# Sign bits of an LSH attention kernel: twelve full-width split matmuls or four narrow fp32 ones, with a new order of all work

## The chip, the cores and the metric

The kernel runs on one core of a Trainium2 chip. The metric is the device time of one execution in microseconds, as the median of several runs. A profiled execution has a time of its own and a span, from its first to its last instruction, in which the trace counts.

## The reference

Four batches of eight heads attend over 768 positions with head dimension 64. A query sees a key only if both fall into the same of 64 buckets; a bucket is the six sign bits of the vector's projection by `proj` (64x6). The attention result, laid side by side over heads, is `x` of a second stage with cosine and sine mixing over tokens and a rectified linear layer.

```python
q_bits = (np.einsum('bhsd,dk->bhsk', q, proj) > 0)      # k_bits alike, from k
mask = q_bucket[:, :, :, None] == k_bucket[:, :, None, :]
scores = np.where(mask, scale * q @ k.T, -1e9)
attn = softmax(scores); x = attn @ v                    # heads side by side
theta = x @ w_theta
y = w_tok_r @ (x * cos(theta)) + w_tok_i @ (x * sin(theta))
u = x + y
out = u + maximum(u @ w_ch, 0)
```

## The kernel before, in words

Work is cut into small operations (`op(...)`) that carry a priority, the engines that may run them and what they depend on. `issue_all` (L111) walks a model of the five engines and gives every engine one list, which it then runs strictly in that order. The priorities come from named constants at the end of the file (L1044 to L1100). A duration in an `op` is the model's and not a measured one.

Heads are worked in pairs; there are sixteen pairs. The steps of a pair that matter here:

- **Load and split** (`prep_qk`, L544). `raw` tiles of q and k, 128 rows (two heads of 64) by 768 positions, come in by DMA (L556). Each is split for exact products into a rounded high part (L563 on ScalarE or L565 on VectorE) and the remainder (L569 on GpSimd or VectorE), both in tile `hl`.
- **Sign bits** (`bits`, L583). `proj` stands, split alike, in four 128x128 tiles `pst` (filled once, L329 and L330), in columns 0 to 23 for q and 32 to 55 for k, each with its negative. TensorE adds three products (high by high, low by high, high by low) for q and three for k into one 128-row PSUM tile `pb`, once for positions 0 to 511 and once for 512 to 767: twelve matmuls in a pair. VectorE makes the bits from rows 0 to 55 with one comparison for each of the two tiles (`rows`, L594). For the very first head it also writes them straight into the operands (L598).
- **Assembly** (`assemble`, L633). SyncE's queue issues six DMAs for a head's `qt` and `kt` operands from `hl` (L640 to L644) and two for its bit rows from `rows` (L648, L649). There are three sets of operands in turn, so a head's assembly waits for the last score matmul of the head three before.
- **Maxima** (`maxima`, L665): matmuls `sq`, a maximum on VectorE (`mc`, L691), a transpose `pmx`, a row sent back by DMA (L715) and a flag row `ft` (L720).
- **Steps** (`step`, L735): score matmuls `st`, the exponential `pf` (L769) and its rounded copy (L775) on ScalarE, the remainder `p` on GpSimd (L781), and products with v into `po`. The matmuls of `po` stream 64 or 65 columns each.

The second stage of a batch (`moe`, L833) is laid between the attention of the next one: `pt_x` and `ps_th` (angles), `py` (token mixing), `pt_u` and `ps_r` (the last layer). For the last batch nothing is left to lay it between. Weights are prepared once, in the first 300 us. All matmuls but the transposes go through the helper `mm`, so their line is L76.

Of the kernel before, what the change touches and what calls it, by code (L numbers as in the profile page):

```python
# [14 lines left out]
F32 = mybir.dt.float32  # L15
# [16 lines left out]
def lsh_attention_moe_kernel(ctx: ExitStack, tc: tile.TileContext, q, k, v, proj, w_theta, w_tok_r, w_tok_i, w_ch, aff, out):  # L32
# [6 lines left out]
    P = 128  # L39
# [30 lines left out]
    for nm in "qk":  # L70
        for part in "hl":
            pst[nm, part] = const.tile([P, P], F32R, name=f"pst_{nm}{part}")
            DVE.memset(pst[nm, part].bitcast(F32), 0.0)
# [10 lines left out]
    SHARED = {"p1", "p2", "zf", "zh", "zl", "mag", "wlow", "whigh", "wmul", "wl", "vv2"}  # L84
# [26 lines left out]
    def issue_all():  # L111
# [96 lines left out]
        while todo:  # L208
            progress = False
            for e in START:  # L210
# [28 lines left out]
                if e == "PE":  # L239
                    dur = pace(now, dur, STREAM.get(o.name, 0.9))  # L240
                elif e == "DVE" and o.name in SHARED:
                    port[0] = max(now, port[1]) + dur
                    dur = port[0] - now
                elif e == "POOL":
                    port[1] = max(now, port[0]) + dur
                    dur = port[1] - now
                elif e == "SP":
                    t_ = now
                    for hold, size in dur:
                        t_ += 25 + hold  # L250
# [48 lines left out]
    def on(e, dur, fn):  # L299
        return {e: (dur, fn)}  # L300
# [21 lines left out]
    def split_proj():  # L322
        for nm, base, first in (("q", 0, 1.0), ("k", 32, -1.0)):
            for j in range(2):
                rows = slice(j * D, (j + 1) * D)
                for n, sgn in enumerate((first, -first)):
                    c0 = base + j * 2 * NB + n * NB
                    h_, l_ = (pst[nm, part][rows, c0 : c0 + NB] for part in "hl")
                    DVE.tensor_scalar(h_, pp[rows, :], sgn, None, ALU.mult)  # L329
                    DVE.scalar_tensor_tensor(l_, pp[rows, :], sgn, h_.bitcast(F32), ALU.mult, ALU.subtract)  # L330

    cload = op("consts", QKL + 0.03, on("SP", [(625, 0)] * 3, load_consts))
    proj_ready = op("pst", QK0, on("DVE", 2200, split_proj), [cload])
# [210 lines left out]
    def prep_qk(b, hp, G, g):  # L544
        t = {}
        sh, sr = Slot("hl"), Slot("rows")
        raws = []
        hs, ls = [], []
        pr = G + at("QK0", b)
        for i, src in enumerate((q, k)):  # L550
            def part(i=i, src=src):
# [25 lines left out]
        fs = []  # L577
        for lo, n_ in ((0, 512), (512, S - 512)):
            def signs(lo=lo, n_=n_):
                sm_ = Slot("m")  # L580
                u = {}

                def bits():  # L583
                    u["pb"] = bank(sm_, [P, 512], f"pb_{b}_{hp}_{lo}")
                    n = 0
                    for i, nm in enumerate("qk"):
                        for a_, c in (("h", 0), ("h", 1), ("l", 0)):
                            mm(u["pb"][:, :n_], pst[nm, a_], t["hl"][:, c, i, lo : lo + n_], n == 0, n == 5)
                            n += 1

                def sign():
                    if "rows" not in t:
                        t["rows"] = ap_.tile([56, S], F32R, tag=sr.tag, bufs=1, name=f"rows_{b}_{hp}")
                    DVE.tensor_scalar(t["rows"][:, lo : lo + n_], u["pb"][:56, :n_], affs[:56, 0:1], affs[:56, 1:2], ALU.is_ge, ALU.mult)  # L594

                def first():
                    for r0, dst in ((0, qts[0]), (32, kts[0])):
                        DVE.tensor_scalar(  # L598
                            dst[MR : MR + NM, 0, lo : lo + n_], u["pb"][r0 : r0 + NM, :n_], affs[r0 : r0 + NM, 0:1], affs[r0 : r0 + NM, 1:2], ALU.is_ge, ALU.mult
                        )  # L600

                b1 = op("bits", G + at("QK1", b), on("PE", 80 + 1340 * n_ / 512, bits), hs + ls + [proj_ready], [sm_, sh])
                if g == 0:
                    t.setdefault("direct", []).append(op("sign0", G + at("QK1", b) - 0.01, on("DVE", 2 * (190 + 540 * n_ / 512), first), [b1], [sm_]))
                fs.append(op("sign", G + at("QK1", b), on("DVE", 190 + 540 * n_ / 512, sign), [b1], [sm_, sr]))

            signs()

        t["parts"], t["bits"], t["slots"] = hs + ls, fs, [sh, sr]
        if g == 0:  # L610
# [10 lines left out]
            t["first"] = list(t["direct"])  # L621
# [11 lines left out]
    def assemble(j, n_, t, prio, free_after):  # L633
        h0 = j * D
        qf, kf = qts[n_].bitcast(F32), kts[n_].bitcast(F32)

        hq, hk = (lambda i=i: t["hl"][:, :, i].bitcast(F32) for i in range(2))

        def parts():
            dma(qf[:D], hq()[h0 : h0 + D, 0:1].to_broadcast([D, 2, S]))  # L640
            dma(kf[:D], hk()[h0 : h0 + D])
            for c in range(2):
                dma(qf[D : D + hd, c], hq()[h0 + c * hd : h0 + (c + 1) * hd, 1])  # L643
                dma(kf[D : D + hd, c], hk()[h0 + c * hd : h0 + (c + 1) * hd, 0])  # L644

        def bits():
            rf = t["rows"].bitcast(F32)
            dma(qf[MR : MR + NM, 0], rf[j * NM : (j + 1) * NM])  # L648
            dma(kf[MR : MR + NM, 0], rf[32 + j * NM : 32 + (j + 1) * NM])  # L649

        n = S * 4
        sh, sr = t["slots"]
        return [
            op("assemble", prio, on("SP", [(1000, 4 * D * n)] * 2 + [(1000, 2 * hd * n)] * 4, parts), t["parts"] + free_after, [sh]),
            op("assbits", prio + AB, on("SP", [(780, NM * n)] * 2, bits), t["bits"] + free_after, [sr]),
        ]
# [383 lines left out]
CL = 0.33  # L1040
# [3 lines left out]
MX0 = -3.263  # L1044
MX1 = 0.411
PIECES = [{1: (0, 3)}, {0: (0, 2), 1: (2, 3)}]
PF = 0.112
KA = 0.401
KB = 0.749
KV = 0.529  # L1050
KN = 1.258
AB = -0.043
WTH = 16.998
WTS = 0.232
WC = 27.543
# [8 lines left out]
TH0_3 = -0.791  # L1064
TH1_3 = 0.535
Y0_3 = 11.712
YS_3 = 4.023
Y1_3 = 0.838
MX0_0 = -3.0
MX1_0 = 0.299  # L1070
AS0_0 = -5.786
PV0_0 = -4.367
QK0_0 = -7.07
QK1_0 = -5.655
HOLD = 0.255
LATE = 6
WL0 = 33.637
WLS = 3.314
TH0_0 = -0.032
TH1_0 = 0.837  # L1080
Y0_0 = 8.598
Y1_0 = 2.702
YS_0 = 4.448
AHEAD = 2.344
QKL = -10.187
QKI = 0.127
QKH = [(0, 999, ["ACT", "DVE"])]
QKLO = [(0, 999, ["POOL", "DVE"])]
QK0 = -5.533
QK1 = -4.662  # L1090
AS0 = -4.539
PV0 = -4.161
LV0 = -5.392
W0 = 0.383
WS = 3.307
TH0 = 0.02
TH1 = 0.742
Y0 = 8.953
YS = 5.502
Y1 = 2.736  # L1100
# [4 lines left out]
def _thresholds(n):  # L1105
# [41 lines left out]
```

## Time and profile before

| | |
|---|---|
| time before, median of 3 runs | 856.34 us (855.6 to 857.42) |
| the profiled execution's own time | 857.2 us |
| its span | 855.4 us |
| mean granted TensorE clock | 0.954 |
| busy: TensorE, VectorE, ScalarE, GpSimd | 794.8, 570.4, 520.9, 497.1 us |
| matmuls of the sign bits | 192 (sixteen pairs by twelve) |

A group line of the profile reads: line, engine, operation, output<-inputs, shapes, count, then busy time and mean duration of one, then the idle time of the engine before them and what ended it. PE is TensorE's matmuls, PEld its weight loads, DVE VectorE, ACT ScalarE, POOL GpSimd and SPq the queue that issues DMAs. Matmuls overlap in the records, so the pace of a row of matmuls is read from start to start and not from durations. A timeline row gives start, length of the merged group, engine, what it is and the count. The chain of waits is the work that ended last, followed back.

### The profile page before, as it was taken

How to read it: one execution, taken by the hardware profiler on the slowest of the kernel's cores; microseconds unless marked ns; L12 is line 12 of the kernel's file. 1: busy time of each engine (PE TensorE's matmuls, PEld its weight loads, DVE VectorE, ACT ScalarE, POOL GpSimd, SP SyncE). 2: the span in 40 equal slices, each digit the busy share in tenths (PEclk: the TensorE clock that was granted, in tenths of full speed). 3: DMA queues.
4: the chain of work that ended last, by engine and by line, in shares of the span. 5: the costliest groups of instructions: out<-in, count | busy, mean ns of one | idle time of the engine just before them, and what ended most of it. 6: DMA issues, size and time to landing. Idle time of an engine off the chain costs nothing.

```text
span 855.4 us, 17719 instructions
## 1 busy us (share of the span) xinstructions
PE 794.8 (93%) x6808; PEld 566.4 (66%) x6808; DVE 570.4 (67%) x962; ACT 520.9 (61%) x888; POOL 497.1 (58%) x511
## 2 busy tenths in 40 slices
PE   3799988899898899999999999999999999999997
PEld 2477766678556676778667766778667766675465
DVE  7999988786898755575896455575796445235413
ACT  3289867777797345467977444476876453657200
POOL 3199976974768545475778544574678543641200
PEclk8599996979899999999999999999999999999999
DMA  7566773753235414344343423252343321000001
GB/s 224 145 194 173 202 180 90 167 130 70 74 81 131 106 41 108 69 100 101 78 93 79 122 53 95 58 134 66 78 93 83 82 47 42 14 14 1 0 21 55
DMA packets 33781, 79.01 MB, mean 92 GB/s; under 512 B 6520, under 2 KB 10808, under 8 KB 33696
## 3 DMA queue, kind: packets, MB, share of 16 engines
q1 hardware_dynamic: 33696, 77.88, 35.8%
q8 instruction: 54, 0.88, 0.4%
q14 instruction: 31, 0.25, 0.1%
HBM read 32.51 MB, written 6.29 MB: 45 GB/s over the span
## 4 chain that ended last, share of the span: by engine, by line
PE 65%; DVE 14%; ACT 9%; SPq 3%; issue 3%; DMA 3%; POOL 3%; DVEq 0%; ACTq 0%; POOLq 0%
PE py L76 18%; PE st L76 12%; PE po L76 9%; PE ps_r L76 8%; PE sq L76 6%; PE ps_th L76 5%; DVE mc L691 3%; PE pb L76 2%; POOL p L781 2%; ACT pf L769 2%; DVE hl L569 2%; ACT p L775 2%; PE pt_u L870 1%; SPq L644 1%; SPq L643 1%
## 5 line engine op out<-in xcount | busy, mean ns | idle before, releaser
L781 POOL TENSOR_TENSOR p<-pf,p 128x512 f16<-128x512 f32 x288 | 357.6, 1263 | 193.5 <-ACT p L775 118.6
L769 ACT ACTIVATE pf<-st 128x512 f32<-128x512 f32 x288 | 164.1, 593 | 132.7 <-PE st L76 123.3
L691 DVE TENSOR_REDUCE mc<-sq 128x1 f32<-128x512 f32 (+1 forms) x288 | 191.1, 681 | 61.9 <-PE sq L76 60.7
L76 PE MATMUL py<-z,wtk 128*128 128x512 f16 x864 | 222.4, 385 | 1.2 <-POOL z L959 0.8
L76 PE MATMUL st<-qt,kt 108*128 108x512 f32 (+3 forms) x768 | 201.1, 378 | 8.1 <-ACT pf L769 7.9
L775 ACT ACTIVATE p<-pf 128x512 f16<-128x512 f32 x288 | 171.8, 628 | 10.7 <-PE po L76 7.7
L76 PEld LDWEIGHTS <-p 128*128 128x128 f16 x3456 | 136.4, 100 | 44.9 <-issue 19.0
L76 PE MATMUL po<-vv,p 128*128 128x65 f16 (+1 forms) x3456 | 158.3, 197 | 6.2 <-POOL p L781 6.1
L76 PE MATMUL sq<-kt,qt 108*128 108x256 f32 (+1 forms) x384 | 137.4, 415 | 21.0 <-DVE mc L691 14.7
L76 PEld LDWEIGHTS st<-qt,kt 108*128 108x128 f32 (+1 forms) x768 | 124.1, 201 | 29.7 <-ACT pf L769 16.2
L76 PEld LDWEIGHTS <-wtk 128*128 128x128 f16 x864 | 71.5, 99 | 86.7 <-issue 26.9
L76 PEld LDWEIGHTS sq<-kt,qt 108*128 108x128 f32 x384 | 70.0, 201 | 45.5 <-DVE mc L691 25.8
L959 POOL TENSOR_TENSOR z<-f,z 128x512 f16<-128x512 f32 x38 | 50.9, 1347 | 49.9 <-ACT z L953 37.4
L948 DVE SCALAR_TENSOR_TENSOR f<-x,zsc,z 128x512 f32<-128x512 f32 x48 | 58.9, 1266 | 9.9 <-ACT z L936 7.3
L76 PE MATMUL ps_th<-wth,h_x 128*128 128x512 f32 x192 | 63.7, 414 | 1.1 <-DVE z L914 0.8
L76 PE MATMUL ps_r<-wch,h_u 128*128 128x512 f32 x192 | 63.3, 411 | 0.8 <-ACT h_u L875 0.7
L994 DVE SCALAR_TENSOR_TENSOR x<-ps_r,x 128x512 f32<-128x512 f32 x24 | 16.6, 691 | 57.3 <-PE ps_r L76 57.3
L875 ACT ACTIVATE h_u<-pt_u 128x512 fp32r<-128x512 f32 x24 | 14.2, 595 | 62.9 <-PE pt_u L870 62.7
L76 PEld LDWEIGHTS ps_th<-wth,h_x 128*128 128x128 f32 x192 | 36.4, 195 | 10.7 <-DVE z L914 1.2
L76 PEld LDWEIGHTS ps_r<-wch,h_u 128*128 128x128 f32 x192 | 35.5, 191 | 9.6 <-ACT h_u L875 0.9
L76 PE MATMUL ps_th<-wth,l_x 128*128 128x512 f32 x96 | 38.9, 406 | 0.1
L76 PE MATMUL ps_r<-wch,l_u 128*128 128x512 f32 x96 | 38.3, 399 | 0.0
(131 smaller groups left out, 935.6 us busy)
## 6 DMA issues: line engine op xcount, KB each, us to landing
qt<-hl SPq DMA_DIRECT2D x31, 384.0 KB
kt<-hl SPq DMA_DIRECT2D x31, 384.0 KB
raw<-in_q_dram SPq DMA_DIRECT2D x16, 384.0 KB
raw<-in_k_dram SPq DMA_DIRECT2D x16, 384.0 KB
vb<-in_v_dram SPq DMA_DIRECT2D x16, 384.0 KB
out_dram<-x SPq DMA_DIRECT2D x24, 256.0 KB
qt<-hl SPq DMA_DIRECT2D x62, 96.0 KB
kt<-hl SPq DMA_DIRECT2D x62, 96.0 KB
```

The costliest lines, as they stand in the source:

```text
L76: PE.matmul(out_, l, r, start=start, stop=stop, skip_group_check=True)
L569: return lambda: eng.tensor_tensor(t["hl"][:, 1, i], t["raw", i], t["hl"][:, 0, i].bitcast(F32), ALU.subtract)
L643: dma(qf[D : D + hd, c], hq()[h0 + c * hd : h0 + (c + 1) * hd, 1])
L644: dma(kf[D : D + hd, c], hk()[h0 + c * hd : h0 + (c + 1) * hd, 0])
L691: DVE.tensor_reduce(col()[:, cs], u["sq"], AX.X, ALU.max)
L769: ACT.activation(wide("pf", spf, F32), u["st"], AF.Exp, scale=1.0 / math.sqrt(D))
L775: ACT.activation(o_, u["pf"], AF.Copy)
L781: return lambda: eng.tensor_tensor(wide("p2", sp2, F16), u["pf"], u["p1"], ALU.subtract)
L875: ACT.activation(u["hi"], u["pt"], AF.Copy)
L948: DVE.scalar_tensor_tensor(u["f"], tl[b][:, tt], zsc[:, b : b + 1], t["zw"][r][:, tt], ALU.mult, ALU.mult)
L959: return lambda: eng.tensor_tensor(t["z"][r, 1][:, tt], u["f"], t["z"][r, 0][:, tt], ALU.subtract)
L994: DVE.scalar_tensor_tensor(tl[b][:, to], r_["ps"], 0.0, tl[b][:, to], ALU.max, ALU.add)
```

## The change

The sign bits no longer use the split tiles. `pst` becomes one plain fp32 tile of 32 columns for q and one for k. Four plain fp32 matmuls read the loaded `raw` tiles, one for each of q and k and each half of 384 positions, and write 32 rows each at partitions 0, 32, 64 and 96 of one PSUM tile. One comparison of 128x384 replaces the two of 56x512 and 56x256. The two halves of the positions now stand in different rows of `rows`, so a head's bits go out in four DMAs of 12x384 instead of two of 12x768. The matmuls wait for the two loads and no longer for the split; in return the `raw` buffers are held until the matmuls have read them.

The planner counts a score or projection matmul that stands behind a short one as dearer, and the lists of all engines are made anew with other priority constants; of those, two lines are shown.

```diff
-        for part in "hl":
-            pst[nm, part] = const.tile([P, P], F32R, name=f"pst_{nm}{part}")
+        pst[nm] = const.tile([P, 32], F32, name=f"pst_{nm}")
...
+        def key(o, e):
+            if e == "PE" and tail_pe in SHORT and o.name in FOUR:
+                return (o.key[0] + PEN, o.key[1])
...
-                    DVE.tensor_scalar(h_, pp[rows, :], sgn, None, ALU.mult)
-                    DVE.scalar_tensor_tensor(l_, pp[rows, :], sgn, h_.bitcast(F32), ALU.mult, ALU.subtract)
+                    DVE.tensor_scalar(pst[nm][rows, c0 : c0 + NB], pp[rows, :], sgn, None, ALU.mult)
...
-                    for i, nm in enumerate("qk"):
-                        for a_, c in (("h", 0), ("h", 1), ("l", 0)):
-                            mm(u["pb"][:, :n_], pst[nm, a_], t["hl"][:, c, i, lo : lo + n_], n == 0, n == 5)
-                    DVE.tensor_scalar(t["rows"][:, lo : lo + n_], u["pb"][:56, :n_], ...)
-                b1 = op("bits", ..., hs + ls + [proj_ready], [sm_, sh])
+            for x in range(2):
+                for i, nm in enumerate("qk"):
+                    r0 = 64 * x + 32 * i
+                    mm(t["pb"][r0 : r0 + 32], pst[nm], t["raw", i][:, x * SH : (x + 1) * SH], True, True)
+            DVE.tensor_scalar(t["rows"], t["pb"], affs[:, 0:1], affs[:, 1:2], ALU.is_ge, ALU.mult)
+        b1 = op("bits", ..., raws + [proj_ready], [sm_] + nats)
...
-            dma(qf[MR : MR + NM, 0], rf[j * NM : (j + 1) * NM])
-            dma(kf[MR : MR + NM, 0], rf[32 + j * NM : 32 + (j + 1) * NM])
+            for x in range(2):
+                for r0, dst in ((64 * x, qf), (64 * x + 32, kf)):
+                    dma(dst[MR : MR + NM, 0, x * (S // 2) : (x + 1) * (S // 2)], rf[r0 + j * NM : r0 + (j + 1) * NM])
...
-AB = -0.043
+AB = 0.151
```

Three places show how the lists move. First, VectorE near its start. `pst` is the projection, `kt` and `qt` are the first head's operands, `vam` is a maximum of v, and `pb` and `affs` stand for the sign operation. Before, these rows follow on fourteen more `pst` rows of the same two kinds:

```order
L329 TENSOR_SCALAR pst_kh<-pp 64x6
L330 SCALAR_TENSOR_TENSOR pst_kl<-pp,pst_kh 64x6
L618 CAST kt_116<-hl_0_141 64x1536
L618 CAST qt_113<-hl_0_141 32x768 x2
L618 CAST kt_116<-hl_0_141 32x768
L453 TENSOR_REDUCE vam_0_189<-vb_0_139 128x1
L598 TENSOR_SCALAR qt_113<-pb_0_0_172,affs 12x512
L598 TENSOR_SCALAR kt_116<-pb_0_0_172,affs 12x512
L594 TENSOR_SCALAR rows_0_203<-pb_0_0_172,affs 56x512
```

Now these are the rows at that place:

```order
L336 TENSOR_SCALAR pst_q<-pp 64x6 x4
L336 TENSOR_SCALAR pst_k<-pp 64x6 x4
L459 TENSOR_REDUCE vam_0_159<-vb_0_135 128x1
L621 CAST kt_112<-hl_0_137 64x1536
L621 CAST qt_109<-hl_0_137 32x768 x2
L621 CAST kt_112<-hl_0_137 32x768
L602 TENSOR_SCALAR qt_109<-pb_0_154,affs 12x384
L602 TENSOR_SCALAR kt_112<-pb_0_154,affs 12x384
```

Eight `pst` operations stand there instead of sixteen, the maximum of v has moved ahead of the copies, and the sign operations still come last.

Second, the queue of DMAs where the fourth head is assembled, `qt_113` with `kt_116` before and `qt_109` with `kt_112` now; `hl` and `rows` are the sources, `vb` is a load of v and `w_t` are loads of the token weights. Before:

```order
L648 DMA qt_113<-rows_1_315 12x768
L649 DMA kt_116<-rows_1_315 12x768
L640 DMA qt_113<-hl_1_250 64x2x768
L641 DMA kt_116<-hl_1_250 64x2x768
L643 DMA qt_113<-hl_1_250 32x768
L644 DMA kt_116<-hl_1_250 32x768
L643 DMA qt_113<-hl_1_250 32x768
L644 DMA kt_116<-hl_1_250 32x768
```

Now:

```order
L643 DMA qt_109<-hl_1_234 64x2x768
L644 DMA kt_112<-hl_1_234 64x2x768
L646 DMA qt_109<-hl_1_234 32x768
L647 DMA kt_112<-hl_1_234 32x768
L646 DMA qt_109<-hl_1_234 32x768
L647 DMA kt_112<-hl_1_234 32x768
L455 DMA vb_2_590<-in_v_dram 128x2x384
L364 DMA w_t_599<-in_moe_w_tok_r_dram 128x1536
L364 DMA w_t_599<-in_moe_w_tok_i_dram 128x1536
L653 DMA qt_109<-rows_1_314 12x384
L653 DMA kt_112<-rows_1_314 12x384
L653 DMA qt_109<-rows_1_314 12x384
```

The bit rows have moved from the head of this assembly to its end, behind three loads, and a fourth of them follows.

Third, TensorE at the end of the program: `pt_u` transposes a block of u, `ps_r` is the last layer on it, from the parts `h_u` and `l_u` and the weights `wch`; blocks are numbered 0 to 5. Before:

```order
L76 MATMUL ps_r_4_11853<-wch_104,h_u_4_11842 128x512
L76 MATMUL ps_r_4_11853<-wch_103,l_u_4_11843 128x512
L870 MATMUL pt_u_5_11867<-ident,x_9159 128x128 x4
L76 MATMUL ps_r_5_11878<-wch_103,h_u_5_11873 128x512
L76 MATMUL ps_r_5_11878<-wch_104,h_u_5_11873 128x512
```

Now:

```order
L75 MATMUL ps_r_2_11703<-wch_100,h_u_2_11671 128x512
L75 MATMUL ps_r_2_11703<-wch_99,l_u_2_11672 128x512
L874 MATMUL pt_u_4_11718<-ident,x_9081 128x128 x4
L874 MATMUL pt_u_5_11724<-ident,x_9081 128x128 x4
L75 MATMUL ps_r_3_11732<-wch_99,h_u_3_11700 128x512
L75 MATMUL ps_r_3_11732<-wch_100,h_u_3_11700 128x512
```

The last transpose has moved ahead of the matmuls of three blocks; before, it stood ahead of those of its own block alone.

More of the change, by code (lines that the diff above doesn't have):

```diff
@@ L70, in lsh_attention_moe_kernel @@
     for nm in "qk":
-        for part in "hl":
-            pst[nm, part] = const.tile([P, P], F32R, name=f"pst_{nm}{part}")
-            DVE.memset(pst[nm, part].bitcast(F32), 0.0)
+        pst[nm] = const.tile([P, 32], F32, name=f"pst_{nm}")
+        DVE.memset(pst[nm], 0.0)
     def mm(out_, l, r, start, stop):
@@ L322, in split_proj @@
     def split_proj():
-        for nm, base, first in (("q", 0, 1.0), ("k", 32, -1.0)):
+        for nm, first in (("q", 1.0), ("k", -1.0)):
             for j in range(2):
@@ L326, in split_proj @@
                 for n, sgn in enumerate((first, -first)):
[L327 to L330, printed above, removed]
+                    c0 = j * 2 * NB + n * NB
+                    DVE.tensor_scalar(pst[nm][rows, c0 : c0 + NB], pp[rows, :], sgn, None, ALU.mult)
     cload = op("consts", QKL + 0.03, on("SP", [(625, 0)] * 3, load_consts))
-    proj_ready = op("pst", QK0, on("DVE", 2200, split_proj), [cload])
+    proj_ready = op("pst", QK0, on("DVE", 700, split_proj), [cload])
     wth = [wp.tile([P, NC, DM], F32R, name=f"wth{i}") for i in range(2)]
@@ new lines, in prep_qk, with bits, sign @@
+        sm_ = Slot("m")
+        SH = S // 2
+        def bits():
+            t["pb"] = bank(sm_, [P, SH], f"pb_{b}_{hp}")
+            for x in range(2):
+                for i, nm in enumerate("qk"):
+                    r0 = 64 * x + 32 * i
+                    mm(t["pb"][r0 : r0 + 32], pst[nm], t["raw", i][:, x * SH : (x + 1) * SH], True, True)
+        def sign():
+            t["rows"] = ap_.tile([P, SH], F32R, tag=sr.tag, bufs=1, name=f"rows_{b}_{hp}")
+            DVE.tensor_scalar(t["rows"], t["pb"], affs[:, 0:1], affs[:, 1:2], ALU.is_ge, ALU.mult)
@@ new lines, in first @@
+        def first():
+            for x in range(2):
+                for r0, dst in ((64 * x, qts[0]), (64 * x + 32, kts[0])):
+                    DVE.tensor_scalar(
+                        dst[MR : MR + NM, 0, x * SH : (x + 1) * SH], t["pb"][r0 : r0 + NM], affs[r0 : r0 + NM, 0:1], affs[r0 : r0 + NM, 1:2], ALU.is_ge, ALU.mult
+                    )
+        b1 = op("bits", G + at("QK1", b), on("PE", 1000, bits), raws + [proj_ready], [sm_] + nats)
+        direct = []
+        if g == 0:
+            direct.append(op("sign0", G + at("QK1", b) - 0.01, on("DVE", 4 * 470, first), [b1], [sm_]))
@@ L609, in prep_qk @@
+        fs = [op("sign", G + at("QK1", b), on("DVE", 570, sign), [b1], [sm_, sr])]
         t["parts"], t["bits"], t["slots"] = hs + ls, fs, [sh, sr]
@@ L619, in copy @@
                 return go
-            t["first"] = list(t["direct"])
+            t["first"] = list(direct)
             pieces = [
@@ L1063 @@
 SEED = 162248
[L1064 to L1075, printed above, removed]
-LATE = 6
[L1077 to L1086, printed above, removed]
+TH0_3 = -0.906
+TH1_3 = 0.619
+Y0_3 = 6.012
+YS_3 = 1.533
+Y1_3 = 0.094
+MX0_0 = -2.821
+MX1_0 = 0.312
+AS0_0 = -3.257
+PV0_0 = -4.336
+QK0_0 = -10.002
+QK1_0 = -6.235
+HOLD = 0.008
+LATE = 6
+WL0 = 17.76
+WLS = -31.029
+TH0_0 = 0.005
+TH1_0 = 0.805
+Y0_0 = 8.965
+Y1_0 = 1.355
+YS_0 = 5.682
+AHEAD = 1.962
+QKL = -12.217
+QKI = 1.196
 QKH = [(0, 999, ["ACT", "DVE"])]
 QKLO = [(0, 999, ["POOL", "DVE"])]
[L1089 to L1100, printed above, removed]
+QK0 = -5.81
+QK1 = -5.002
+AS0 = -1.218
+PV0 = -4.271
+LV0 = -3.122
+W0 = -0.514
+WS = 3.131
+TH0 = -0.21
+TH1 = 0.948
+Y0 = 8.868
+YS = 5.812
+Y1 = 2.817
 _INS = ["q", "k", "v", "proj", "moe_w_theta", "moe_w_tok_r", "moe_w_tok_i", "moe_w_ch"]
```

76 lines of the change are left out of this document (32 added, 44 removed).

## The prediction

> **What bounds the kernel now.** I read the page's busy shares first, then the windows by stretch, then the chain of waits.
>
> ```profile
> PE 794.8 (93%) x6808; PEld 566.4 (66%) x6808; DVE 570.4 (67%) x962; ACT 520.9 (61%) x888; POOL 497.1 (58%) x511
> ```
>
> ```profile
> 0.00:24.00 24.00, 9.46 (x25) 5.91 (x25) 19.30 (x50) 8.48 (x8) 7.85 (x20) 0.82 0.67 200
> 24.00:290.00 266.00, 234.33 (x2150) 175.06 (x2150) 232.64 (x371) 202.36 (x353) 199.48 (x193) 0.88 0.52 137
> 290.00:760.00 470.00, 462.33 (x4205) 331.70 (x4203) 281.76 (x494) 279.67 (x484) 278.08 (x291) 0.99 0.32 77
> 760.00:856.00 96.00, 88.67 (x432) 53.73 (x432) 36.73 (x49) 30.41 (x44) 11.66 (x9) 1.00 0.05 17
> ```
>
> The columns behind the stretch are its length and the busy time of PE, PEld, DVE, ACT and POOL, then the granted clock. From 290 to 760 us TensorE is busy for 462.33 of 470 us (98%) and the others for about 60%: a microsecond taken off TensorE there is a microsecond off the end. From 24 to 290 us TensorE has 88%, VectorE 87%, at a clock of 0.88: two engines share the bound. In the first 24 us VectorE leads with 19.30.
>
> ```profile
> PE 65%; DVE 14%; ACT 9%; SPq 3%; issue 3%; DMA 3%; POOL 3%; DVEq 0%; ACTq 0%; POOLq 0%
> ```
>
> The chain agrees: two thirds TensorE, and VectorE mostly at the start.
>
> **The sign-bit matmuls, old price.** Sixteen pairs; the same windows for tile `pb` alone give twelve matmuls in the first stretch, 72 in the second, 108 in the third, so one, six and nine pairs.
>
> ```profile
> 0.00:24.00 24.00, 3.93 (x12) 2.99 (x12) 4.02 (x6) 0.82 0.67 200
> 24.00:290.00 266.00, 16.00 (x72) 12.20 (x72) 7.71 (x12) 0.88 0.52 137
> 290.00:760.00 470.00, 22.66 (x108) 17.45 (x108) 11.81 (x18) 0.99 0.32 77
> ```
>
> A pair at full clock, from TensorE's timeline, with what follows it:
>
> ```profile
> 590.06 0.62 PE L76 MATMUL pb<-hl,pst_qh 128*128 128x512 f32 x2
> 590.53 0.40 PE L76 MATMUL pb<-hl,pst_ql 128*128 128x512 f32 x1
> ...
> 591.80 0.40 PE L76 MATMUL pb<-hl,pst_kh 128*128 128x256 f32 x2
> 592.04 0.28 PE L76 MATMUL pb<-hl,pst_kl 128*128 128x256 f32 x1
> 592.16 0.60 PE L870 MATMUL pt_x<-ident,x 128*128 128x128 f32 x4
> ```
>
> From 590.06 to 592.16 is 2.10 us a pair. A 256-column matmul takes 0.12 us of it from start to start (591.80 to 592.04 for two).
>
> **New price.** No row shows a plain fp32 matmul of 32 output columns. The nearest is `pm`, plain fp32 with 33 output columns over 128 streamed ones.
>
> ```profile
> L76 PE MATMUL pm<-vb,ones x32: 272/297/425, 25.2 to 695.8; 128*33 128x128 f32 x32
> L76 PEld LDWEIGHTS pm<-vb,ones x32: 107/110/161, 25.2 to 695.7; 128*33 128x33 f32 x32
> 51.94 0.41 PE L76 MATMUL pm<-vb,ones 128*33 128x128 f32 x2
> ```
>
> There are 32 records for sixteen calls (one a pair), so a plain fp32 matmul is two instructions. The two together last 0.41 us and one lasts 0.297, so the second starts 0.113 us after the first: 128 columns take what 256 take in the split form. For 384 columns that is 0.34 us an instruction, and a pair has eight. If nothing overlaps, a pair takes 8 x 0.34 = 2.7 us, 0.6 more than now. If the four narrow matmuls, which write separate quarters of the partitions, run beside each other, it takes 2 x 0.34 = 0.68 us. If they start strictly in list order, and only the second instruction of each must wait for its first, the steps are five: 1.7 us. I take 1.2 us, the middle of the two overlapping cases, since the four share no output rows and wait for one another in nothing that the diff shows; that they overlap at all is shown by no row, and the other end is a rival below.
>
> The Trainium skill ("TensorE: Matmul & The Clock Gate", Part 3, "Measured speedup vs the span model") states 2.38 times for three column tiles of 32. By it four would give some 3.2 times, an estimate: 0.85 us a pair, and 837 us for the whole; no row here shows it.
>
> **What the saving is worth.** 2.1 - 1.2 = 0.9 us a pair. Nine pairs count in full; six lie where VectorE binds as much as TensorE, and I count half; the first one belongs to the start. That is 12 x 0.9 = 10.8 us off, and between 17 off (0.68) and 7 on (2.7).
>
> **VectorE.** One comparison for two, and fewer preparations.
>
> ```profile
> L594 DVE TENSOR_SCALAR rows<-pb,affs 56x512 fp32r<-56x512 f32 x16 | 12.8, 797 | 10.9 <-PE pb L76 10.8
> L594 DVE TENSOR_SCALAR rows<-pb,affs 56x256 fp32r<-56x256 f32 x16 | 8.5, 529 | 2.6 <-PE pb L76 2.6
> ```
>
> Between 529 ns for 256 and 797 for 512, 384 columns take 0.66; a pair goes from 1.33 to 0.66. After 290 us VectorE's idle 40% hides that; before, it is in the half that I counted. At the start it is on the path, first by its timeline, then by the chain:
>
> ```profile
> 5.68 0.16 DVE L329 TENSOR_SCALAR pst_qh<-pp 64x6 fp32r<-64x6 f32 x1
> ...
> 9.90 0.16 DVE L330 SCALAR_TENSOR_TENSOR pst_kl<-pp,pst_kh 64x6 fp32r<-64x6 f32 x1
> 10.09 0.95 DVE L618 CAST kt<-hl 64x1536 fp32r<-64x1536 f32 x1
> ...
> 12.67 0.95 DVE L453 TENSOR_REDUCE vam<-vb 128x1 f32<-128x768 f32 x1
> 13.66 0.80 DVE L598 TENSOR_SCALAR qt<-pb,affs 12x512 fp32r<-12x512 f32 x1
> ```
>
> ```profile
> 37.24 2.82 PE pwt L424 x12
> ```
>
> VectorE works without a break from 5.68, and in the chain it stays the main carrier up to the first weight transposes. Sixteen `pst` operations take 5.68 to 10.09, 4.4 us; eight at 0.19 from start to start (9.90 to 10.09) take 1.5, so 2.9 us go. The four direct sign operations keep their sum (twice 797 and twice 529 before, four times 660 now). The comparisons of the first two pairs give 0.67 each. Together 4.2; I take 4 us. New on the path could be the first bits themselves:
>
> ```profile
> 8.70 1.19 PE L76 MATMUL pb<-hl,pst_qh 128*128 128x512 f32 x2 [8.70 <-DVE pst_qh L329]
> ...
> 12.35 0.28 PE L76 MATMUL pb<-hl,pst_kl 128*128 128x256 f32 x1
> ```
>
> At that clock the pair takes 3.9 us, 1.87 times 2.1. With `pst` done at 7.2, bits of 1.2 x 1.87 = 2.2 us end at 9.4, while the copies and the maximum of v hold VectorE until 10.7: hidden. At 2.7 x 1.87 = 5.1 they end at 12.3, and 1.6 of the 4 us is lost.
>
> **The new order on TensorE.** A wide weight load behind short matmuls shows:
>
> ```profile
> 492.16 0.71 PE L76 MATMUL st<-qt,kt 108*128 108x512 f32 x2
> 492.70 0.63 PE L76 MATMUL pb<-hl,pst_qh 128*128 128x512 f32 x2
> ```
>
> Behind `po`, the two `st` take 0.54 us; two `pb` in a dense stream took 0.47 (590.06 to 590.53). So 0.07 us at each such place. The lists have 231 of them before; now 200, and eight more behind the new bits: 23 fewer, 1.6 us off. At the end the last block:
>
> ```profile
> 847.00 0.60 PE L870 MATMUL pt_u<-ident,x 128*128 128x128 f32 x4
> ...
> 848.29 0.73 PE L76 MATMUL ps_r<-wch,h_u 128*128 128x512 f32 x2 [0.69 <-ACT h_u L875]
> ...
> 849.01 0.50 PE L76 MATMUL ps_r<-wch,l_u 128*128 128x512 f32 x1
> ```
>
> TensorE idles 0.69 us ahead of the block's first matmul, and the third comes 0.72 after it where 0.47 is usual: 0.9 us of waiting for the split of u. Now the matmuls of two more blocks, 24 of 0.23 us, lie between that transpose and this block, 5.6 us in which the split is done, and the 0.9 goes. What else the new constants move I count as zero.
>
> **SyncE's queue.** Two more DMAs for each of 31 heads:
>
> ```profile
> 410.68 0.77 SPq L648 DMA_DIRECT2D qt<-rows  x1
> 411.51 0.72 SPq L649 DMA_DIRECT2D kt<-rows  x1
> ```
>
> The first and the last of four heads whose assembly is in the chain of waits, how long `sq` waited for bit rows, and what the `raw` loads wait for:
>
> ```profile
> 89.51 1.22 SPq L643
> ...
> 325.49 1.22 SPq L643
> ```
>
> ```profile
> L76 PE MATMUL sq<-kt,qt 108*128 108x512 f32 x192 | 91.4, 493 | 11.5 <-DVE mc L691 8.3 <-DVE kt L598 1.5 <-DMA kt<-rows 1.2
> ```
>
> ```profile
> SPq L556 <- DVE hl L569: 67.1, 13, 13.3
> ```
>
> One costs 0.8 us with its gap, so an assembly takes 1.6 us longer, and where the bits now come last, behind loads, the first `sq` of the head waits for that; the row and flag DMAs of other heads stand behind it. The cost lies between nothing, since `sq` waited 1.2 us on `rows` in the whole run, and 31 x 1.6 = 50. If the four heads in the chain all stay there, it is 6.4 us. TensorE idles for only 7.7 us from 290 to 760, so most of the 6.4 is covered by other work; I take 2 us. The `raw` loads get one more reader to wait for, TensorE, with the rest of the queue behind them; they already wait 67.1 us for the remainders on VectorE, which read the same tile, so I cost that at nothing; without this cover, a load comes later by TensorE's lag behind the split.
>
> **Sum.** -10.8 - 4 - 1.6 - 0.9 + 2 = -15.3. The profiled execution's own time is 857.2, its span 855.4 and 1.8 around it, which stays; 841.9. It lies 0.9 above the median shown, so 841 us.
>
> **Rivals.**
> - *Nothing overlaps (slower).* The eight instructions of a pair run one behind another: 12 x (2.7 - 1.2) = 18, and 1.6 at the start: 860.6. It decides when a pair costs over 1.2 + 15.3 / 12 = 2.5 us. For it: no row shows two matmuls beside each other. If besides no weight load were hidden, 8 x 0.11 (the `pm` load) add 0.9 a pair, 871. Against that last part:
>
> ```profile
> L76 PEld LDWEIGHTS pb<-hl,pst_qh x64: 187/190/339, 8.7 to 686.4; 128*128 128x128 f32 x64
> ```
>
>   Loads of 0.19 us would bring twelve matmuls to over 4 us a pair, and they took 2.10: the loads are hidden, though all use the full 128 rows. The Trainium skill (the same page and part, "The mechanism") has it that a weight load overlaps a running matmul only if their row groups differ; the trace speaks against it.
> - *The queue is late.* If eight of the heads assembled before 290 us each lose 1.6 us, 12.8 stands for my 2: 852. For it: bits at the end of an assembly; against: the 1.2 us.
> - *The order gives it back.* If the new lists lose the 2.5 us of the two order terms and double TensorE's 7.7 us of idling, it is 851.
>
> **How the numbers follow.** Overlap, 0.65: 835 (0.68 us a pair) to 847 (1.7), likeliest 841. Nothing overlaps, 0.13, of which 0.02 at 871. Queue, 0.10. Order, 0.12. The range is 830 to 857: the overlap case with some microseconds for the order either way, and both cases at 851 and 852; it leaves out nearly all of the slow rival and a few hundredths below. A measurement can tell about 0.2%, 1.7 us. Faster by more: 0.65, and most of the queue and order cases with a little of the slow one, 0.20, together 0.85. Same: 0.05. Slower: 0.10, from the slow rival.
>
> **What would show it.** Right: `pb` from its first start to the next matmul takes about 1.2 us at full clock, with starts nearer together than 0.34; VectorE reaches the first sign operation some 3 us before 13.66; the gap ahead of the last `ps_r` is gone; TensorE is still at 98% from 290 us on. Wrong: eight `pb` records at 0.34 us from start to start, `sq` rows idle behind DMAs from `rows`, or more idle TensorE from 290 us to the last batch's second stage than 8 us.

## The result and the profile after

| | before | after |
|---|---|---|
| median of the runs | 855.97 us (4 runs, 854.99 to 857.42) | 831.0 us (4 runs, 829.88 to 832.03) |
| profiled execution: own time, span | 857.2, 855.4 us | 829.88, 827.8 us |
| TensorE idle in the span | 60.6 us | 59.8 us |

The ratio of after to before is 0.9707, 95% interval 0.9686 to 0.9727: 25.0 us faster, where 15.3 were forecast. The time lies in the range, 1 us inside its fast end.

The busy times of the engines over the whole span of after:

```profile
PE 768.0 (93%) x6744; PEld 532.5 (64%) x6744; DVE 562.5 (68%) x940; ACT 519.4 (63%) x889; POOL 497.8 (60%) x506
```

TensorE went from 794.8 us to 768.0, 26.8 off, and its idle time stayed. Almost the whole difference of the spans, 27.6, is TensorE's busy time.

The windows of after by stretch. The columns are the length, the busy time of PE, PEld, DVE, ACT and POOL, the granted clock, the share of the DMA engines and GB/s:

```profile
0.00:24.00 24.00, 8.87 (x22) 3.87 (x23) 19.20 (x40) 10.08 (x11) 10.18 (x21) 1.00 0.70 200
24.00:290.00 266.00, 240.48 (x2240) 170.19 (x2239) 223.62 (x364) 198.50 (x351) 199.00 (x189) 0.93 0.49 134
290.00:733.00 443.00, 429.95 (x4044) 304.35 (x4041) 283.09 (x489) 280.13 (x485) 276.88 (x288) 1.00 0.34 84
733.00:828.00 95.00, 88.73 (x448) 54.12 (x446) 36.60 (x49) 30.64 (x45) 11.70 (x9) 1.00 0.05 17
```

From 24 to 290 us TensorE now has 90% (88% before), VectorE 84% (87%), and the granted clock reads 0.93 for 0.88 (it leaves something out at the start, as the last section shows). In the long middle TensorE has 97%, so it is still the bound, with 13.1 us idle there where it was 7.7. The same windows for the sign-bit tile `pb` on TensorE alone, the first column behind the length being the busy time:

```profile
0.00:24.00 24.00, 2.02 (x8) 1.00 0.70 200
24.00:290.00 266.00, 5.90 (x48) 0.93 0.49 134
290.00:760.00 470.00, 7.67 (x72) 1.00 0.32 79
```

The sum fell from 42.59 us to 15.60. That is 27.0 off, so in the sum the rest of TensorE's work takes what it took. One pair, by TensorE's timeline of after, with what follows it:

```profile
470.29 0.51 PE L75 MATMUL pb<-raw,pst_q 128*32 128x384 f32 x1
470.30 0.51 PE L75 MATMUL pb<-raw,pst_k 128*32 128x384 f32 x1
470.30 0.51 PE L75 MATMUL pb<-raw,pst_q 128*32 128x384 f32 x1
470.31 0.51 PE L75 MATMUL pb<-raw,pst_k 128*32 128x384 f32 x1
470.63 0.49 PE L75 MATMUL pb<-raw,pst_q 128*32 128x384 f32 x1
...
470.65 0.49 PE L75 MATMUL pb<-raw,pst_k 128*32 128x384 f32 x1
471.07 0.82 PE L75 MATMUL py<-z,wtk 128*128 128x512 f16 x3
```

Four instructions start within 0.02 us, and 0.34 us later four more: the four strips run side by side, one instruction of each, then the other. From the first to the `py` behind them are 0.78 us, where a pair took 2.10.

VectorE's start, by its timeline:

```profile
5.67 2.16 DVE L336 TENSOR_SCALAR pst_q<-pp 64x6 f32<-64x6 f32 x4
7.87 0.49 DVE L336 TENSOR_SCALAR pst_k<-pp 64x6 f32<-64x6 f32 x4
...
11.82 0.67 DVE L602 TENSOR_SCALAR qt<-pb,affs 12x384 fp32r<-12x384 f32 x1
```

The first sign operation came 1.84 us earlier than before's 13.66, not 3: the eight `pst` operations take 5.67 to 8.36, since the first four hold 2.16 us and not 0.8.

The end, on TensorE:

```profile
814.55 1.04 PE L874 MATMUL pt_u<-ident,x 128*128 128x128 f32 x8
815.35 0.71 PE L75 MATMUL ps_r<-wch,h_u 128*128 128x512 f32 x2
...
823.63 0.39 PE L75 MATMUL ps_r<-wch,l_u 128*128 128x512 f32 x1
```

No row there carries idle time any more: the 0.9 us ahead of the last block is gone. And what TensorE waited for on the queue (in all, how often, the longest), where before it was 1.2 us once:

```profile
PE sq L75 <- DMA kt<-rows: 4.0, 4, 2.3
```

### The profile page after: what moved, and what is told of

The parts are those of the page before. It is cut to its first block, busy times and chain, and to the rows that moved or that the text cites. A ratio compares the mean times of both kernels' runs of the same rounds, so it can differ in the third digit from the quotient of the medians.

```text
span 827.8 us, 17652 instructions
## 1 busy us (share of the span) xinstructions
PE 768.0 (93%) x6744; PEld 532.5 (64%) x6744; DVE 562.5 (68%) x940; ACT 519.4 (63%) x889; POOL 497.8 (60%) x506
## 5 line engine op out<-in xcount | busy, mean ns | idle before, releaser
L785 POOL TENSOR_TENSOR p<-pf,p 128x512 f16<-128x512 f32 x288 | 361.5, 1279 | 174.6 <-ACT p L779 131.4
L695 DVE TENSOR_REDUCE mc<-sq 128x1 f32<-128x512 f32 (+1 forms) x288 | 191.8, 684 | 61.6 <-PE sq L75 59.8
L75 PE MATMUL py<-z,wtk 128*128 128x512 f16 x864 | 217.1, 380 | 0.3 <-POOL z L963 0.2
L75 PE MATMUL st<-qt,kt 108*128 108x512 f32 (+3 forms) x768 | 198.5, 373 | 13.8 <-ACT pf L773 13.4
L75 PEld LDWEIGHTS <-p 128*128 128x128 f16 x3456 | 134.5, 100 | 38.7 <-issue 17.3
L75 PE MATMUL sq<-kt,qt 108*128 108x512 f32 (+1 forms) x384 | 132.2, 408 | 24.1 <-DVE mc L695 13.7
L75 PEld LDWEIGHTS st<-qt,kt 108*128 108x128 f32 (+1 forms) x768 | 121.6, 195 | 38.7 <-ACT pf L773 25.6
L952 DVE SCALAR_TENSOR_TENSOR f<-x,zsc,z 128x512 f32<-128x512 f32 x48 | 56.8, 1226 | 9.4 <-ACT z L940 7.1
L75 PEld LDWEIGHTS ps_th<-wth,h_x 128*128 128x128 f32 x192 | 34.9, 188 | 11.4 <-DVE z L918 1.8
L991 DVE SCALAR_TENSOR_TENSOR x<-py,sw,x 128x512 f32<-128x512 f32 x24 | 17.8, 743 | 32.8 <-PE py L75 32.8
```

Source lines behind the costliest of these rows:

```text
L75: PE.matmul(out_, l, r, start=start, stop=stop, skip_group_check=True)
L695: DVE.tensor_reduce(col()[:, cs], u["sq"], AX.X, ALU.max)
L785: return lambda: eng.tensor_tensor(wide("p2", sp2, F16), u["pf"], u["p1"], ALU.subtract)
L952: DVE.scalar_tensor_tensor(u["f"], tl[b][:, tt], zsc[:, b : b + 1], t["zw"][r][:, tt], ALU.mult, ALU.mult)
L991: DVE.scalar_tensor_tensor(tl[b][:, to], res["py"], t["sw"][:, to : to + 1], tl[b][:, to], ALU.mult, ALU.add)
```

## The experiments

Each changes after, if nothing else is said. The theory that came out of the result, theory 1: the time follows TensorE's work, so most of the 25 us comes from the sign bits' price, which fell further than I took, and from VectorE's shorter start. Its rival: the new order and a warmer clock brought more than half. Where an expectation has theories with letters, it says itself what they hold. Where a median is set against after's 831.0, it is from another set of runs; the ratios go by the before of its own set.

### The two halves of the change apart

The new bits with the planner's rules and constants of before:

```
-CL = 0.333
+CL = 0.33
...
-AB = 0.151
+AB = -0.043
```

> The narrow sign-bit matmuls with the planner rules and constants of before; the lists are made anew for the changed operations only. Theory 1 (the time follows TensorE's work: sixteen pairs at 2.10 us became 0.78, and VectorE's start is shorter): most of the 25 us is here, 832 to 838 us. Rival (the new order and the warmer clock brought more than half of the gain): 843 to 850 us.

Measured: 843.56 us (842.09 to 844.76), ratio 0.9861, interval 0.9839 to 0.9883. The page's busy times:

```profile
PE 772.7 (92%) x6744; PEld 530.1 (63%) x6744; DVE 562.8 (67%) x937; ACT 518.6 (62%) x889; POOL 498.9 (59%) x509
```

TensorE's busy time falls by 22.1 us, but of its span of 842.0 TensorE idles 69.3 us, 8.7 more than before. What it waits for most is the reduction that gives the maximum of the scores, where after has 13.7 us on it:

```profile
PE sq L75 <- DVE mc L689: 22.9, 26, 2.6
```

So the bits alone bring half of the gain, 12 us; on a list that was chosen for other durations part of their saving turns into waits. The time lies in the rival's range and outside theory 1's. But a warmer clock is not what sets after apart from this run: the mean here is 0.979, in after 0.977.

The other half, as an edit of before: its split bits in the rules and constants of after, so that the planner orders the old work by the new numbers.

```
+            if e == "PE" and tail_pe in SHORT and o.name in FOUR:
+                return (o.key[0] + PEN, o.key[1])
...
-CL = 0.33
+CL = 0.333
...
-AB = -0.043
+AB = 0.151
```

> The split sign bits of before with the planner rules and constants of the changed kernel. Theory 1: 850 to 857 us, within some microseconds of before. Rival: 838 to 846 us, with a granted clock near the 0.977 of the changed kernel rather than the 0.954 of before.

Measured: 862.94 us (861.68 to 864.24), ratio 1.0088, interval 1.0066 to 1.0111. That is slower than either text had it, at a mean clock of 0.956: the new constants by themselves, on the old work, cost 7 us. The two halves alone give -12 and +7, together -25: they don't add, so neither "bits" nor "order" is a term that can be priced alone.

### The price of the bits on a fixed list

The lists of the engines stay as in after in the next five, but for the instructions that an edit names. First the strips are taken away: four plain fp32 matmuls of 128 output columns add into the same rows. For that `pst` grows to 192 columns, with zeros around the 24 that it fills, and `c0` picks the 128 that put each product into its rows.

```
-                    mm(t["pb"][r0 : r0 + 32], pst[nm], t["raw", i][:, x * SH : (x + 1) * SH], True, True)
+                    mm(t["pb"], pst[nm][:, c0 : c0 + P], t["raw", i][:, x * SH : (x + 1) * SH], x + i == 0, x + i == 2)
```

> The changed kernel with the same lists, but the four fp32 matmuls are 128 columns wide and add into the same rows, so they cannot run beside each other. Expected 2.7 us a pair instead of 0.78 in every theory. Theory 1: each of sixteen pairs costs 1.9 us more and twelve to sixteen of them count, 854 to 862 us. Rival (much of the bits' price hides beside other waits): under 846 us.

Measured: 852.99 us (849.97 to 855.79, 10 runs), ratio 0.9975, interval 0.9954 to 0.9996. A pair on TensorE's timeline, its first and last two of eight instructions:

```profile
486.66 0.89 PE L75 MATMUL pb<-raw,pst_q 128*128 128x384 f32 x2
...
488.67 0.81 PE L75 MATMUL pb<-raw,pst_k 128*128 128x384 f32 x2
489.32 0.81 PE L75 MATMUL py<-z,wtk 128*128 128x512 f16 x3
```

From 486.66 to 489.32 are 2.66 us: the 2.7 of the rival "nothing overlaps", measured. It costs 1.88 a pair more than after and 22.0 us in all (22.9 by the ratios), which is 11.7 to 12.2 pairs' worth; the time is 1 us under theory 1's range and far above the rival's. Two things follow. My 12 pairs were right as a sum; which pairs count in full, this run doesn't show. And the rival "nothing overlaps", on this list, lands at 853 and not at 860.6: not slower than before, since something else in the change brings some 10 us.

Then the narrow matmuls are issued twice:

```
-            for x in range(2):
+            for x in (0, 1, 0, 1):
```

> The changed kernel with the same lists; the four narrow matmuls are issued twice, the second time over the first's result, 0.70 us more a pair. e3_wide gave 22.0 us for 1.88 us a pair, 11.7 pairs' worth. If the worth is the same for a small change: 8 us more, 839 us. If only the nine pairs after 290 us count: 837. If all sixteen do: 842.

Measured: 839.12 us (834.46 to 839.69), ratio 0.978, interval 0.9746 to 0.9814; 8.1 us over after. The window of the nine last pairs for `pb` on TensorE:

```profile
290.00:760.00 470.00, 14.33 (x144) 0.99 0.32 80
```

Nine pairs take 14.33 us for 7.67, 0.74 more each. So 8.1 us are 10.9 pairs' worth, or 11.6 at the 0.70 that was expected. By the ratios (0.978 and 0.9707) it is 6.2 us, and either figure has some 3 us of noise: this agrees with the wide form, but can't tell nine pairs from twelve. With the 11.7 of the wide form, the step from 2.10 to 0.78 is worth 1.32 x 11.7 = 15.4 us on this list. That is an estimate on a straight line from 0.78 to 2.66, good to some 2 us; no run had 2.10 on this list.

### The start of VectorE, and the queue

Eight more small operations on VectorE between the `pst` operations, written to a tile that nothing reads:

```
+                    DVE.scalar_tensor_tensor(junk[rows, c0 : c0 + NB], pp[rows, :], sgn, pst[nm][rows, c0 : c0 + NB], ALU.mult, ALU.subtract)
```

> The changed kernel with the same lists; eight more small operations on VectorE (into a scratch tile that nothing reads) stand between the eight that prepare pst, as many as before the change. If VectorE's start carries to the end: 1.5 us more at 0.19 each, 832 to 834 us. If other waits of the first 40 us cover it: 831 us, no difference beyond the interval.

Measured: 832.73 us (829.99 to 833.53), ratio 0.9707, interval 0.9676 to 0.9737: not to be told from after. The 1.5 us in question is less than the interval, so the time rules neither text out, and the traces have to tell. VectorE of this kernel, at the first sign operation and at the first batch's first normalization:

```profile
13.48 0.67 DVE L604 TENSOR_SCALAR qt<-pb,affs 12x384 fp32r<-12x384 f32 x1
```

```profile
63.12 0.60 DVE L831 SCALAR_TENSOR_TENSOR x<-po,vinv,rc 128x384 f32<-128x384 f32 x1
```

And the second of them in after:

```profile
63.49 0.60 DVE L829 SCALAR_TENSOR_TENSOR x<-po,vinv,rc 128x384 f32<-128x384 f32 x1
```

The first sign operation comes 1.66 us later than in after, and by 63 us nothing of it is left. By these traces the start doesn't carry to the end in the new list. (One of the operations lasts 1.8 us; the last section comes back to it.)

For the queue, two comparisons of 64x384 in place of one of 128x384, which lets a head's bits go out in two DMAs as before:

```
-            DVE.tensor_scalar(t["rows"], t["pb"], affs[:, 0:1], affs[:, 1:2], ALU.is_ge, ALU.mult)
+            for x in range(2):
+                r = slice(64 * x, 64 * x + 64)
+                DVE.tensor_scalar(t["rows"][:, x * SH : (x + 1) * SH], t["pb"][r], affs[r, 0:1], affs[r, 1:2], ALU.is_ge, ALU.mult)
...
+            for r0, dst in ((0, qf), (32, kf)):
+                dma(dst[MR : MR + NM, 0], rf[r0 + j * NM : r0 + (j + 1) * NM])
```

> The changed kernel with the same lists; two comparisons of 64x384 put both halves of the positions into the same rows, and two DMAs instead of four carry a head's bits. If the longer queue costs TensorE (it waited 4.0 us for bit rows): 826 to 829 us. If the queue is covered and VectorE's 0.66 us more a pair is what counts: 831 to 835 us. Theory 1 takes the second, near 831.

Measured: 835.42 us (833.74 to 838.09), ratio 0.977, interval 0.9742 to 0.9797; 4.4 us over after and just above the 831 to 835 of the covered queue. The waits of `sq` for bit rows are no longer among the larger ones, and instead VectorE runs 32 comparisons for 16, at the same 0.67 us each:

```profile
L599 DVE TENSOR_SCALAR rows<-pb,affs 64x384 fp32r<-64x384 f32 x32 | 21.6, 674 | 5.6 <-PE pb L75 5.3
```

The 10.8 us of VectorE (10.8 in after, 21.6 here) cost more than the two DMAs a head bring. It changes two things at once, so it bounds the queue's cost and doesn't give it. The other way, eight DMAs of 12x192:

```
-            for x in range(2):
...
+            for x in range(4):
+                for r0, dst in ((64 * (x // 2), qf), (64 * (x // 2) + 32, kf)):
...
```

> The changed kernel with the same lists; a head's bit rows go out in eight DMAs of 12x192 instead of four of 12x384, so each assembly takes some 3.2 us longer in the queue. If the queue is covered: 830 to 834 us. If it is on the path of the eleven heads that are assembled in the first 290 us: 11 x 3.2 = 35, at least half of it seen, 848 us or more.

Measured: 853.47 us (849.1 to 856.06, 10 runs), ratio 0.9968, interval 0.9946 to 0.9991; 22 us over after, as the text for a queue on the path had it. What TensorE waits for on the queue in this kernel (`rows` are bit rows, `row` is the row that `maxima` sends back):

```profile
PE sq L75 <- DMA kt<-rows: 7.0, 4, 3.4
...
PE st L75 <- DMA qt<-row: 5.5, 5, 2.0
...
PE sq L75 <- DMA qt<-rows: 1.9, 1, 1.9
```

These are 14.4 us for 4.0 in after. TensorE's idle time rises by 16 us (851.1 less 775.3 is 75.8, for 59.8), its busy time by 7.3. An assembly that is 3.2 us longer is late for TensorE; the 1.6 us that the change itself added showed as 2.8 us of such waits (4.0 for 1.2).

### How much hangs on the list

A random addition of at most 0.05 to each priority makes another list by the same rules. No operation changes.

```
-JIT = 0
+JIT = 0.05
```

> The changed kernel; every priority gets a random addition of up to 0.05, so that the planner makes other lists from the same constants. e1_bits_alone is 12.5 us behind the changed kernel with the same operations. If that is the worth of the broad choices in the constants (when weights and assemblies come): 829 to 835 us. If it is the fit of one particular list: 838 to 848 us.

Measured: 870.37 us (865.96 to 873.74), ratio 1.0153, interval 1.0108 to 1.0199: 39 us slower than after, beyond what either text had, and slower than before. With another draw (`SEED` 2):

> After, with another random addition of at most 0.05 to each priority. Theory A (any neighbour of the chosen list is worse): again slower than after by 15 to 45 us, 846 to 876. Theory B (the first disturbed list was an unlucky one): within 10 us of after, 822 to 841.

Measured: 872.47 us (870.75 to 872.98), ratio 1.0206, interval 1.0181 to 1.023: 41 slower. And the same done to the kernel before:

> The kernel before, with a random addition of at most 0.05 to each priority of the planner, so that its list is another one made by the same rules and constants; no operation is changed. Theory A (each list is fitted to its prices by choosing constants among many, and any neighbour of it is worse by some tens of us): before with its list disturbed is slower than before by 15 to 45 us, as the disturbed list of after was by 39. Theory B (only the list of after stands at such a lucky place, before's is an ordinary one): 0 to 10 us slower or faster, 850 to 866.

Measured: 892.96 us (892.18 to 896.45), ratio 1.0451, interval 1.0422 to 1.048: 37 us slower than before. All three disturbed lists lose about 40 us: the 15 to 45 of theory A in the two latter texts, and the first draw was not an unlucky one. Disturbed against disturbed, the change is worth 20 to 23 us (870.37 and 872.47 against 892.96), nearly its 25, by two draws of after and one of before.

Where such a list loses them shows at the border between two batches. The windows of the first disturbed list in steps of 10 us:

```profile
400.00:410.00 10.00, 6.58 (x32) 4.00 (x31) 9.89 (x16) 9.94 (x13) 3.56 (x3) 0.71 0.58 122
410.00:420.00 10.00, 9.02 (x28) 5.64 (x27) 8.40 (x10) 7.27 (x14) 9.22 (x8) 0.61 0.16 45
```

The same border in after:

```profile
390.00:400.00 10.00, 7.82 (x35) 4.84 (x34) 7.46 (x10) 9.96 (x16) 4.50 (x4) 1.00 0.72 166
400.00:410.00 10.00, 9.96 (x114) 7.47 (x115) 9.87 (x13) 9.94 (x19) 10.00 (x8) 1.00 0.01 2
```

In steps of 1 us, TensorE alone, the disturbed list shows where its clock changes (length, busy time, clock):

```profile
403.00:404.00 1.00, 0.72 (x4) 1.00 0.97 200
404.00:405.00 1.00, 0.92 (x2) 0.61 0.97 203
405.00:406.00 1.00, 0.99 (x3) 0.50 0.97 200
...
417.00:418.00 1.00, 1.00 (x4) 0.57 0.00 0
418.00:419.00 1.00, 1.00 (x6) 1.00 0.00 0
```

And TensorE's timeline in that stretch:

```profile
402.61 1.10 PE L75 MATMUL sq<-kt,qt 108*128 108x512 f32 x3 [0.70 <-DVE mc L695]
403.89 2.10 PE L75 MATMUL sq<-kt,qt 108*128 108x512 f32 x4 [0.18 <-DVE mc L695]
...
408.46 0.73 PE L75 MATMUL po<-vv,p 128*128 128x65 f16 x10 [1.75 <-POOL p L785]
...
415.59 1.05 PE L75 MATMUL ps_th<-wth,h_x 128*128 128x512 f32 x2
...
416.87 1.05 PE L75 MATMUL ps_th<-wth,h_x 128*128 128x512 f32 x2
```

After idles 2.2 us in its ten and the clock stays at 1.00. In the disturbed list the clock halves at 404.2, behind waits of 0.70 and 0.18 us, and comes back at 417.9 (a mean of 0.61 over a microsecond is 0.78 us at a half, one of 0.57 is 0.86). In between TensorE waits more, up to 1.75 us at once, and what it does goes slower: the three matmuls from 415.59 to 416.87 take 1.28 us where 0.70 is usual. It does 60 matmuls in 20 us (32 and 28) where after does 149 (35 and 114), over half of them the short ones of `po`. The second draw has the same place at 0.71 and 0.60. Over the whole span the granted clock leaves out 4.7% of 864.1, 40.6 us, where after's leaves out 2.3% of 827.8, 19.0; the difference of 21.6 is close to the 19.3 us that TensorE's busy time rose with the same instructions (787.3 for 768.0). So about half of the 36.3 us by which this span is longer fits TensorE at half clock behind or amid waits, and the rest is the waits themselves (17.0 us more idle). It isn't half in every such list: the second draw has 17.9 us more of busy time and 23.3 more of idle time than after, and the disturbed list of before 11.4 and 24.2 more than before.

Two smaller steps away from the list of after. First, eight of the constants put back to before's, those by which the preparation of the token weights and the splits of the other weights fall due (some 350 rows of TensorE differ):

```
-WTH = 18.491
+WTH = 16.998
...
-WLS = -31.029
+WLS = 3.314
```

> After, with the planner's eight weights and offsets of before put back, and its prices and the rest of the new constants kept; some 350 rows of TensorE's list differ. If what the order brings is a fit of one list (theory A), the time goes up by 5 to 25 us, to 836 to 856. If the gain comes from the new bits' price alone and the weights are worth nothing (theory B), it stays within 3 us of after, 828 to 834.

Measured: 841.13 us (835.19 to 842.18), ratio 0.9823, interval 0.9784 to 0.9862: some 10 us slower than after, within what its theory A has; that the weights are worth nothing is out. Its profiled execution, with a span of 833.1, is the fastest of its runs, so its trace doesn't show the loss.

Second, without the penalty that keeps `po` and the transposes away from `st`, `sq` and the projections:

```
-            if e == "PE" and tail_pe in SHORT and o.name in FOUR:
+            if e == "PE" and False and tail_pe in SHORT and o.name in FOUR:
...
```

> After, without the new penalty by which the planner keeps two kinds of matmuls apart; some 870 rows of TensorE's list differ. Theory A (fit of one list): 5 to 25 us slower than after, 836 to 856, with more idle time of TensorE rather than more busy time. Rival (the rule itself saves TensorE time at each change of kind): TensorE's busy time rises by over 5 us and idle time stays. Theory B (rule worth nothing): 828 to 834.

Measured: 842.89 us (837.68 to 847.07), ratio 0.9855, interval 0.9809 to 0.99: some 12 us slower. The page, for a span of 841.4:

```profile
PE 774.5 (92%) x6744; PEld 534.7 (64%) x6744; DVE 560.2 (67%) x942; ACT 518.0 (62%) x886; POOL 498.6 (59%) x507
```

TensorE's busy time rises by 6.5 us and its idle time by 7.1. Both rose, and neither expectation holds alone. The list has 236 places where a wide load stands behind short matmuls for after's 200; at my 0.07 us that is 2.5 of the 6.5. But the mean clock is 0.969 for 0.977, which leaves out 26.1 us of the span for 19.0, so the rise of the busy time can as well come from there.

## Why the prediction was right, and where its sizes were off

The direction and its main mechanism were right; the sum was 10 us short, 5 of it in one term and 5 in the rest. Both misses went the same way, and that the time still lies in the range, by 1 us, is luck.

- **The new price of a pair** was mis-sized. I took 1.2 us, the middle between strips side by side (0.68) and starts in list order (1.7). Measured: 0.78, nearly the end of the range, with all four strips starting within 0.02 us. The estimate of 0.85 from the Trainium skill ("TensorE: Matmul & The Clock Gate", Part 3, "Measured speedup vs the span model") came nearer than my choice; wide against narrow, the runs show 2.66 to 0.78, 3.4 times.
- **The worth of twelve pairs** was right as a sum: 11.7 to 12.2 by the wide form, and the matmuls issued twice agree within their noise. The term is about -15.4 where the forecast had -10.8.
- **VectorE's start** was mis-sized, -4 us. I took 1.5 us for the eight `pst` operations that stay; they take 2.7, since one of them lasts 1.9 us. Before's timeline has such a row as well (1.81 us from 5.87), and I priced it like the others. The first sign operation came 1.84 us earlier. And the experiment that gives 1.66 of it back costs nothing that can be told from after. The chain of before led through the start of before's list; in after's the time there is absorbed by 63 us. On this list the term lies between 0 and some -2, as closely as the runs tell.
- **The gap at the end** went as forecast: from the last head's normalization to the end of the span the profiles have 89.2 us before and 88.2 after.
- **Fewer exposed weight loads** (-1.6) wasn't measured by itself. The run without the penalty has 36 more such places and is slower, but its clock is lower too, so it gives the term no size.
- **SyncE's queue** (+2): 2.8 us more of `sq` waiting for bit rows is what the trace shows. The step that "most of it is covered" held at 1.6 us an assembly and would not have held at twice that, as the 22 us for four more DMAs show.
- **"What else the new constants move I count as zero"** was the step with the least ground. Of the 25 us, some 15.4 are the bits' price on a fixed list; 9.6 are left, where the forecast had 4.5, and no run gives these 5 us to one cause. Other draws and other constants make this kernel 10 to 40 us slower, so an order is worth that much. But both kernels stand on lists that fit them, and disturbed they lose nearly alike (37 us, and 39 and 41): most of it cancels, and 2 to 5 us do not. The rival "the order gives it back" had the mechanism but only one sign and a price of 10.
- **Of the signs named**, two went against the forecast without turning the result: TensorE has 97% and not 98% in the middle, with 13.1 us of idle time where I had set the mark at 8 us, and `sq` does wait behind DMAs from `rows`.

What stays open is how the 9.6 us divide. The granted clock reads higher (0.977 for 0.954 over the span), about half of which the start explains, as the last section shows. It went with the bits and not with the constants (0.979 and 0.956 in the two halves of the change); TensorE's busy time apart from `pb` is the same in both traces (752.2 and 752.4 us); and no run held the list and moved the clock alone. VectorE's saving from one comparison for two, away from the start, was bounded only together with the queue: 4.4 us for 10.8 us more of it.

## What to carry to other kernels

When several small fp32 matmuls write separate strips of 32 partitions, price them as running side by side and look for starts within hundredths of a microsecond; here the four took 0.78 us, little more than the 0.68 of one of them. A change of durations under an automatic order is two changes: to size one, hold the list and move one price by a known amount (here by 1.88 and by 0.74 us a pair), and to size the other, disturb both lists and compare them. A gain found on one list may be half as large, or lost, on the next.

## What the runs showed of the hardware

- Four plain fp32 matmuls with 32 output columns each, at partitions 0, 32, 64 and 96, all streaming 128 rows, are eight instructions: the first ones of all four start within 0.02 us, the second ones 0.34 us later. In the program's first pair the starts fall apart, three steps instead of two:

```profile
7.89 0.85 PE L75 MATMUL pb<-raw,pst_q 128*32 128x384 f32 x1 [7.89 <-DVE pst_q L336]
8.41 0.85 PE L75 MATMUL pb<-raw,pst_k 128*32 128x384 f32 x1
...
9.07 0.85 PE L75 MATMUL pb<-raw,pst_k 128*32 128x384 f32 x1
```

  An instruction takes 0.85 us there for 0.51 in the middle of the program, though the granted clock of that stretch reads 1.00. The second pair has the same, with 0.64 us between its first and second instructions:

```profile
31.71 0.85 PE L75 MATMUL pb<-raw,pst_q 128*32 128x384 f32 x1
...
32.35 0.85 PE L75 MATMUL pb<-raw,pst_q 128*32 128x384 f32 x1
```

  So TensorE ran at about half pace until about 33 us in after, and by its `pb` rows until about 12 us in before, and the column reads 1.00 in both stretches. Counted at a half, they leave out some 17 and 6 us more, an estimate. That takes about 10 of the 20 us by which the two means of 0.977 and 0.954 differ, so the means can't be compared without a look at the rows.
- The granted clock in these traces is either 1.00 or 0.50, and it stays low for whole multiples of one length: 13.64 us in the stretch above (404.22 to 417.86), and in the same way 10.24 us from 602.18 and, in after, 6.84 us from 156.16. These are 4, 3 and 2 times 3.41 to 3.42. The Trainium skill ("TensorE: Matmul & The Clock Gate", Part 1, "What's actually happening") has the gate decide in free-running windows of 3413 ns; the trace agrees to some hundredths. The same page ("HAM oscillation — how this bites in real kernels") has the rule that idle gaps of over 3.4 us bring the clock down; here it fell behind gaps of 0.70 and 0.18 us at one place, and in after didn't fall beside 2.2 us in three pieces. Whether the gap's place in such a window decides was not tried.
- One of the small VectorE operations of 64x6 lasts 1.8 or 1.9 us, where the others take 0.15 to 0.24. In thirteen of the fourteen traces it is the one that starts beside GpSimd's subtraction in the split, and it ends within 0.2 us of that. By the timeline of before:

```profile
5.85 1.80 POOL L569 TENSOR_TENSOR hl<-raw,hl 128x768 fp32r<-128x768 f32 x1 [0.92 <-ACT hl L563]
5.87 1.81 DVE L330 SCALAR_TENSOR_TENSOR pst_ql<-pp,pst_qh 64x6 fp32r<-64x6 f32 x1
7.60 0.22 DVE L329 TENSOR_SCALAR pst_qh<-pp 64x6 fp32r<-64x6 f32 x1
```

  There it is the second operation. In after it is the third, a `pst_q` of another kind, from 5.91 to 7.82 beside GpSimd's from 5.85 to 7.66. In the disturbed list of before GpSimd's starts at 7.24, and the eleventh operation, from 7.32, lasts 1.92 us. In the first disturbed list of after GpSimd does nothing of the kind there, and no operation is long:

```profile
5.77 0.48 DVE L336 TENSOR_SCALAR pst_q<-pp 64x6 f32<-64x6 f32 x4
```

  So it isn't a price of the operation, and multiplying the count by one duration missed it. That the one engine holds up the other is read from these traces; no run moved GpSimd's operation by itself.
